# Loading the w_in groups by eight transfers that alternate between the partition halves

## The chip, the core and the metric

The kernel runs on one core of a Trainium2 chip. The metric is the device time of one execution in microseconds (us). The kernel before takes 523.92 us, the median of three runs (523.12 to 524.32).

## What is computed

An mLSTM cell (4 batches, 8 heads, 768 steps, head width 40) is followed by a feed-forward block with the activation h·cos(h). The two parts are joined by a reshape: 3,072 tokens of 320 values.

```python
for t in range(S):                        # _attn_ref, per batch and head
    m_new = np.maximum(f_gate[:, :, t] + m, i_gate[:, :, t])
    ...
    C = f_stab * C + i_stab * outer(vt, kt)
    n = f_stab * n + i_stab * kt
    y[:, :, t] = sigmoid(o_gate[:, :, t]) * (C @ qt) / np.maximum(np.abs(n @ qt), 1.0)
x = attn_out.transpose(0, 2, 1, 3).reshape(B * S, H * D)
h = x @ w_in                              # 3072x320 by 320x2048
out = (h * np.cos(h)) @ w_out             # 2048x320
```

The two weight matrices arrive as 64-bit floats. The kernel makes 32-bit floats of them on the chip, by work on the bits.

## The kernel before

**Work and order.** The steps are cut into six chunks of 128 (`c`), and a cell is one batch of one chunk, so there are 24 cells. `first_cells` does the four cells of chunk 0 and starts the weights. After that the cells of chunk c+1 are done in between the feed-forward products of chunk c. These products go by pairs of hidden tiles: `f2` from 0 to 7, each with two tiles of 128 hidden units (`e` = 0, 1). `Up(c, f2)` multiplies the chunk's 512 tokens by the pair's columns of w_in (L726 and L720 in chunk 0), the activation follows (`near` L733 on ScalarE, `rest` L736 on VectorE, `sin` L741 on ScalarE, `gate` L745 on VectorE), and `down` multiplies the result by the pair's rows of w_out (L757). In later chunks both products run in half arrays (L670). The order is written out by hand (`first_cells`, `first_period`, `both_parts`), and each engine goes through its instructions in that order.

**Weights.** `weights_in(f)` fetches one of four groups of w_in, 512 columns, for two `f2`. The 320 rows of w_in are 8 heads of 40. The first 32 rows of the heads go to the tile `bits` (128 partitions, 2 slots i, 512 columns of 8 bytes): four transfers (L180), one for each 32 partitions `a`, each with both slots, 64 rows of 4,096 bytes, 256 KB. The last 8 rows of the heads, 64 rows in all, go to the tile `low`: the even tile of a pair to partitions 0 to 63, the odd one to 64 to 127, by four transfers (L185) of 64 rows of 1,024 bytes. `weights_in` returns three pieces: slot 0, slot 1 and low. Each piece is turned into floats by `take_apart` (ScalarE, L158 and L160), `bound` (VectorE, L164 and L165) and `put_together` (VectorE L171, then GpSimd L172). `weights_out(p)` fetches two tiles of w_out by one transfer of 640 KB to all 128 partitions (L191), which is turned by the same functions. The f-th group is asked for at L987, L1047, L1076 and L1143. The second w_out piece, the one that `down(0, 1)` needs, is asked for at L1066, behind group 1, the load of E for cell 5 (L1064) and the eight transfers of the output gate (`load_o(1)`, L1065).

**Transfers.** Nearly all transfers are issued by SyncE (SP), in program order. Until cell 6 or so (`at_once`), `transfer` issues at once (L320). The DMA completions of SP are counted on eight semaphores that take turns, so an issue can stand behind the landing of the transfer eight places earlier. `load_o(c)` fetches the output gate by eight transfers, two (`g`) for each 32 partitions `a`. `load_E(n)` fetches the decay exponents, 128 partitions of 4,096 bytes, and, for even cells, `G` by two transfers of 64 partitions.

Of the kernel before, what the change touches and what calls it, by code (L numbers as in the profile page):

```python
# [12 lines left out]
I32 = mybir.dt.int32  # L13
# [16 lines left out]
def kernel(  # L30
# [20 lines left out]
    nc = tc.nc  # L51

    B, H, S, D = q.shape
# [3 lines left out]
    HP = H // 2  # L57
# [6 lines left out]
    NK = DM // 128  # L64
# [71 lines left out]
    w_in_sb = wp.tile([128, NK, DFF], FP, name="w_in_sb")  # L136
# [5 lines left out]
    WP, WQ = 512, 2 * DM  # L142
    w_out_bits = moe_w_out.bitcast(I32).rearrange("r (n two) -> r n two", two=2)
    w_in_heads = moe_w_in.bitcast(I32).rearrange("(a e d) m -> a d e m", e=NK, d=D)
# [27 lines left out]
        nc.gpsimd.tensor_tensor(out=t, in0=t, in1=m, op=OP.add)  # L172


    w_in_last = moe_w_in.bitcast(I32).rearrange("(h d) (a e n) -> e a h d n", d=D, e=2, n=2 * 128)[:, :, :, 32:D]

    def weights_in(f):
        bits = pb.tile([128, NK, WP, 2], I32, name="bits", tag="bits")
        for a in range(HP):
            nc.sync.dma_start(out=bits[32 * a:32 * a + 32].rearrange("r i n two -> r i (n two)"),  # L180
                              in_=w_in_heads[a, 0:32, :, ts(f, 2 * WP)])
        low = p2.tile([128, 2 * 128, 2], I32, name="low", tag="S")
        for e in range(2):
            for a in range(2):
                nc.sync.dma_start(out=low[64 * e:64 * e + 64, ts(a, 128)].rearrange("r n two -> r (n two)"), in_=w_in_last[e, 2 * f + a])  # L185
        return [(w_in_sb[:, i, ts(f, WP)], bits[:, i]) for i in range(NK)] + [(w_in_l[:, ts(f, 2)].rearrange("p a n -> p (a n)"), low)]


    def weights_out(p):
        bits = pc.tile([128, 2, DM, 2], I32, name="bits", tag="bits")  # L190
        nc.sync.dma_start(out=bits, in_=w_out_bits[ts(p, 256)].rearrange("(e r) n two -> r e n two", e=2))  # L191
        return w_out_sb[:, ts(p, 2)].rearrange("p f n -> p (f n)"), bits.rearrange("p e n two -> p (e n) two")


# [100 lines left out]
    sig, xT, xL, Es, kws, qkT, pss, heads_of, raw_o, Gs, early = {}, {}, {}, {}, {}, {}, {}, {}, {}, {}, {}  # L295
# [16 lines left out]
    def transfer(out, in_, room=4):  # L312
        todo.append((out, in_, room))
        if at_once[0]:
            issue(None)

    def issue(room):
        while todo and (room is None or todo[0][2] <= room or todo[0][2] == ROOM <= room + 8):
            dst, src, took = todo.pop(0)
            nc.sync.dma_start(out=dst, in_=src)  # L320
            if room is not None:
                room -= took

    def load_o(c, bs=range(B)):
        if c == 0:
            sig[c] = og.rearrange("q b k i -> q (b k i)")[:, 0:B * DM].rearrange("q (b h d) -> q b h d", b=B, h=H)
            for b in bs:
                nc.sync.dma_start(out=sig[c][:, b], in_=o_gate[b, :, ts(c, C)].rearrange("h t d -> t h d"))
            return
        raw_o[c] = p1.tile([128, B, 2 * C // 32, D], FP, name="o", tag="o")  # L330
        src = o_gate.rearrange("b (a g) (c t k) d -> a g c t b (k d)", g=2, k=C // 32, t=32)
        for a in range(HP):
            for g in range(2):
                dst = raw_o[c][32 * a:32 * a + 32].rearrange("t b (g k) d -> t g b (k d)", g=2)[:, g]
                transfer(out=dst, in_=src[a, g, c], room=6)
# [329 lines left out]
    def both(low, high, done):  # L665

        passed = max(bank.seen if bank.half == 1 - half else 0 for half, bank, *_ in (low, high))
        for half, bank, a, lhs, rhs, start, stop in (low, high):
            r = slice(64 * half, 64 * half + 64)
            ins = nc.tensor.matmul(a, lhs[r], rhs[r], start=start, stop=stop).ins  # L670
            if passed:
                tc.add_manual_dep(ins, over[passed - 1].name, SYNC, reason="a bank passes from one half to the other")
            bank.half, bank.seen = half, len(over) + 1
        if done:
            over.append(nc.sync.nop().ins)
            tc.add_manual_dep(over[-1], ins.name, SYNC, reason="the halves are done with their banks")
# [5 lines left out]

    spare_bank = 1

    class Up:


# [6 lines left out]
        def split(self, c, f2):  # L694
            banks = [Bank(pu) for pu in self.pu]

            def product(half, e, i, start=False):
                pu = self.pu[e]
                if i < NK:
                    return (half, banks[e], pu.rearrange("p (b t) -> p b t", b=B), w_in_sb[:, i, ts(2 * f2 + e, 128)],  # L700
                            xT[c][:, i:NK * B:NK], start, False)
                return half, banks[e], pu, w_in_l[:, f2], xL[c].rearrange("p b t -> p (b t)"), False, True

            for i in range(NK):
                both(product(0, 1, i, i == 0), product(1, 0, i, i == 0), i == NK - 1)
            if f2 == 3:
                send_kept()
            apart(c, f2)
            issue(24 if f2 % 2 else 32)
            for i in range(NK + 1):  # L710
                both(product(0, 0, i), product(1, 1, i), False)

        def whole(self, c, f2):

            ahead = f2 % 2 == 1 and c < NC - 1

            def low():
                for e, pu in enumerate(self.pu):
                    r = slice(64 * e, 64 * e + 64)
                    nc.tensor.matmul(pu, w_in_l[r, f2], xL[c][r].rearrange("p b t -> p (b t)"), start=ahead, stop=not ahead)  # L720

            if ahead:
                low()
            for i in range(NK):
                for e, pu in enumerate(self.pu):
                    nc.tensor.matmul(pu.rearrange("p (b t) -> p b t", b=B), w_in_sb[:, i, ts(2 * f2 + e, 128)], xT[c][:, i:NK * B:NK],  # L726
                                     start=(i == 0 and not ahead), stop=(i == NK - 1 and ahead))
            if not ahead:
                low()
# [50 lines left out]
    def send_kept():  # L780
        while kept:
            dst, src = kept.pop(0)
            transfer(out=dst, in_=src, room=5)
# [135 lines left out]
    def apart(c, f2):  # L919

        if f2 == 1 and c > 1:
            late_of[c - 1] = late_products(c - 1)
            run(late_of[c - 1], 2)
        else:
            d = c if f2 else c - 1
            run_to(d, done[d] + (2 if c in (1, NC - 1) or f2 % 2 else 3))
# [28 lines left out]
    def first_cells():  # L955
# [5 lines left out]
        load(0, "v")  # L961
        load(1, "qk")
        load_o(0, (0, 1))
        load(1, "v")
        load(2, "qk")
# [17 lines left out]
        load(2, "v")  # L983
        load_E(3)
        load_o(0, (2, 3))
        load(3)
        pieces.extend(weights_in(0))  # L987
        wall_in(1, 0, psum_o())
        wall_in(1, 1, psum_o())
# [36 lines left out]
        seam(1)  # L1026
        load_two(B, "Kv")
        outs.append((0, weights_out(0)))
        weigh(2)
        decay_exponents(3)  # L1030
# [14 lines left out]
        put_together(*pieces.pop(0))  # L1045
        values(3)
        pieces.extend(weights_in(1))  # L1047
        seam_out(2)
        state(2)
# [13 lines left out]
        put_together(*pieces.pop(0))  # L1063
        load_E(B + 1)  # L1064
        load_o(1)  # L1065
        outs.append((1, weights_out(1)))  # L1066
        load_E(B + 2)
        outs.append((2, weights_out(2)))
        low_dimensions(B)
        turn_blocks(B)  # L1070
# [3 lines left out]
        odd_values(B)  # L1074
        scale_q(B)
        ahead.append(weights_in(2))  # L1076

    spot = const.tile([1, 1], FP, name="spot")
# [240 lines left out]
```

## Time and profile before

| | us |
|---|---|
| median of three runs | 523.92 |
| the profiled execution | 523.49 |
| its span, first to last instruction | 521.4 |
| around the span (523.49 - 521.4) | 2.1 |
| PE busy | 500.7 (96% of the span) |
| DVE, ACT, POOL busy | 405.1, 285.5, 247.6 |
| mean granted PE clock | 0.991 |

PE is TensorE's matmuls, PEld its weight loads, DVE is VectorE, ACT ScalarE, POOL GpSimd, SP SyncE and SPq its queue of DMA issues. In the waits, "A <- B: x, n, y" says that A stood idle for x us in n places, y at the longest, until B. In the timelines the columns are start, duration, engine, line, operation, tiles, count, and in brackets the idle time before and what ended it. In the view by stages, each row has the length, each engine's busy time, the granted PE clock, the DMA engines' busy share and GB/s. Besides these views the trace keeps each DMA packet with its start, size and duration; 16 DMA engines work side by side.

The transfers named above, in the page's list:

```profile
E<-M_d SPq DMA_DIRECT2D x22, 512.0 KB, 3.9
...
bits<-in_moe_w_out_dram SPq DMA_DIRECT2D x8, 640.0 KB, 4.4
bits<-in_moe_w_in_dram SPq DMA_DIRECT2D x16, 256.0 KB, 7.7
```

The last column is the median time from issue to landing in us.

### The profile page before, as it was taken

The page shows a single profiled execution, that of the slowest core. Times are in us where ns is not written, and L with a number is a line of the kernel's source. Part 1 is how long each engine was busy: PE and PEld are TensorE (multiplying, and loading weights), DVE is VectorE, ACT ScalarE, POOL GpSimd, SP SyncE. Part 2 cuts the span into 40 slices and gives each one's busy share as a digit, 9 for nine tenths or more (in the row PEclk, how much of TensorE's full clock was granted, in tenths as well). Part 3 has the DMA queues.
Part 4 walks back from the last instruction along what each step waited for, and adds up shares of the span by engine and source line. Part 5 has one row for each costly group of instructions (what it writes and reads, how often), then busy time and mean ns, then how long its engine had stood idle before and what let it go on. Part 6 is the DMA issues. An engine that isn't in the chain of part 4 may idle for free.

```text
span 521.4 us, 14075 instructions
## 1 busy us (share of the span) xinstructions
PE 500.7 (96%) x5568; PEld 360.6 (69%) x5568; DVE 405.1 (78%) x826; ACT 285.5 (55%) x547; POOL 247.6 (47%) x411
## 2 busy tenths in 40 slices
PE   6999869899999999999999999999999999999995
PEld 3874446555667877877767777767787677677775
DVE  4888589897778887898887898877888778654644
ACT  2797498767575446836437837437827532222230
POOL 7536455555665866544564544563432433122212
PEclk9999988999999999999999999999999999999998
DMA  9999899999721645543534454634563000001001
GB/s 138 216 190 190 209 224 213 250 188 240 136 97 31 140 80 145 121 69 90 137 93 115 100 119 112 161 80 105 123 110 106 1 7 6 1 1 52 1 1 52
DMA packets 97777, 58.04 MB, mean 111 GB/s; under 512 B 62048, under 2 KB 89792, under 8 KB 97712
## 3 DMA queue, kind: packets, MB, share of 16 engines
q1 hardware_dynamic: 95952, 55.31, 49.5%
q0 software_dynamic: 1424, 1.49, 1.2%
q8 instruction: 44, 0.72, 0.6%
q10 hardware_dynamic: 336, 0.34, 0.2%
q14 instruction: 21, 0.17, 0.1%
HBM read 51.71 MB, written 4.11 MB: 107 GB/s over the span
## 4 chain that ended last, share of the span: by engine, by line
PE 81%; DMA 10%; DVE 3%; SPq 1%; POOL 1%; issue 1%; ACT 1%; DVEq 0%; POOLq 0%
PE pup L670 32%; PE acc L670 24%; DMA bits<-in_moe_w_in_dram 4%; PE late L670 4%; PE ps L499 3%; PE po L757 3%; DMA E<-M_d 3%; PE pup L726 3%; PE vt L534 2%; PE vt L525 2%; DMA ks<-in_k_dram 2%; DMA qr<-in_q_dram 1%; PE pu L626 1%; PE pup L720 1%; PE pw L953 1%
## 5 line engine op out<-in xcount | busy, mean ns | idle before, releaser
L733 ACT ACTIVATE n<-pup 128x512 int32<-128x512 f32 x96 | 52.3, 593 | 182.1 <-PE pup L670 165.8
L670 PE MATMUL pup<-xT,w_in_sb 64*128 64x512 f32 x608 | 148.2, 596 | 0.2 <-DVE g L745 0.2
L736 DVE SCALAR_TENSOR_TENSOR n<-pup,n 128x512 f32<-128x512 f32 x96 | 61.9, 686 | 73.3 <-ACT n L733 73.2
L670 PEld LDWEIGHTS pup<-xT,w_in_sb 64*128 64x128 f32 x608 | 60.1, 187 | 35.0 <-issue 31.8
L811 POOL TENSOR_TENSOR D<-g 128x128 f32<-128x128 f32 x40 | 18.9, 472 | 132.1 <-DVE g L745 122.8
L741 ACT ACTIVATE n<-n 128x512 f32<-128x512 f32 x96 | 58.9, 630 | 17.5 <-DVE n L736 17.5
L670 PE MATMUL acc<-w_out_sb,g 64*128 64x160 f32 x624 | 63.7, 297 | 0.0
L745 DVE SCALAR_TENSOR_TENSOR g<-pup,n 128x512 f32<-128x512 f32 x96 | 62.2, 681 | 1.4
L670 PE MATMUL acc<-T,g 64*128 64x160 f32 x624 | 61.7, 296 | 0.0
L670 PEld LDWEIGHTS acc<-w_out_sb,g 64*128 64x128 f32 x624 | 55.7, 187 | 8.3 <-issue 8.1
L670 PEld LDWEIGHTS acc<-T,g 64*128 64x128 f32 x624 | 54.1, 187 | 9.6 <-issue 8.9
L632 POOL DMA_DIRECT2D xL<-xT x40 | 22.4, 561 | 63.9 <-DVE xT L562 49.5
L430 ACT ACTIVATE E<-E,tab 128x128 f32<-128x128 f32 x160 | 49.0, 388 | 0.2
L757 PE MATMUL po<-w_out_sb,g 128*128 128x320 f32 x128 | 37.6, 449 | 3.7 <-POOL w_out_sb L172 3.7
L670 PE MATMUL pup<-xL,w_in_l 64*128 64x512 f32 x152 | 40.3, 589 | 0.0
L670 PE MATMUL acc<-T,S 64*128 64x160 f32 x312 | 39.5, 296 | 0.0
L670 PE MATMUL acc<-w_out_sb,S 64*128 64x160 f32 x312 | 39.2, 296 | 0.0
L726 PE MATMUL pup<-xT,w_in_sb 128*128 128x512 f32 x80 | 36.8, 602 | 1.5 <-DVE g L745 1.4
L757 PEld LDWEIGHTS po<-w_out_sb,g 128*128 128x128 f32 x128 | 24.9, 197 | 16.2 <-POOL w_out_sb L172 4.5
L499 PEld LDWEIGHTS ps<-t,t 40*128 40x128 f32 (+1 forms) x384 | 25.3, 188 | 11.3 <-DVE t L480 5.7
L670 PEld LDWEIGHTS acc<-w_out_sb,S 64*128 64x128 f32 x312 | 30.4, 187 | 3.1 <-issue 3.1
L670 PEld LDWEIGHTS late<-w_out_sb,D 64*128 64x128 f32 x320 | 28.7, 187 | 4.9 <-issue 4.2
(199 smaller groups left out, 958.6 us busy)
## 6 DMA issues: line engine op xcount, KB each, us to landing
E<-M_d SPq DMA_DIRECT2D x22, 512.0 KB, 3.9
qr<-in_q_dram SPq DMA_DIRECT2D x36, 160.0 KB, 3.6
kr<-in_k_dram SPq DMA_DIRECT2D x36, 160.0 KB, 5.5
G<-G_d SPq DMA_DIRECT2D x20, 256.0 KB, 5.6
bits<-in_moe_w_out_dram SPq DMA_DIRECT2D x8, 640.0 KB, 4.4
bits<-in_moe_w_in_dram SPq DMA_DIRECT2D x16, 256.0 KB, 7.7
out_dram<-o_sb SPq DMA_DIRECT2D x22, 160.0 KB, 3.8
ks<-in_k_dram SPq DMA_DIRECT2D x10, 320.0 KB, 7.1
```

Source lines behind the costliest of these rows:

```text
L430: nc.scalar.activation(out=Es[n][:, h], in_=Es[n][:, h], func=AF.Exp, scale=-1.0, bias=tab[:, c, 0, g:g + 1])
L499: nc.tensor.matmul(ps[j][:, p], kT[r, p], qT[r, p], start=True, stop=True)
L525: nc.tensor.matmul(vt[32 * a:32 * a + 32, i], vs(n)[:, h, 0:32], E[:, h], start=True, stop=False)
L632: nc.gpsimd.dma_start(out=xL[c][64 * e:64 * e + 64, b], in_=ys[n][0:128:2])
L670: ins = nc.tensor.matmul(a, lhs[r], rhs[r], start=start, stop=stop).ins
L726: nc.tensor.matmul(pu.rearrange("p (b t) -> p b t", b=B), w_in_sb[:, i, ts(2 * f2 + e, 128)], xT[c][:, i:NK * B:NK], start=(i == 0 and not ...
L733: nc.scalar.activation(out=self.n[e], in_=self.pu[e], func=AF.Copy, bias=0.25)
L736: nc.vector.scalar_tensor_tensor(out=self.n[e].bitcast(FP), in0=self.pu[e], scalar=0.25, in1=self.n[e], op0=OP.add, op1=OP.subtract)
L741: nc.scalar.activation(out=r, in_=r, func=AF.Sin, scale=TWO_PI_DOWN)
L745: nc.vector.scalar_tensor_tensor(out=g, in0=self.pu[e], scalar=TWO_PI, in1=self.n[e].bitcast(FP), op0=OP.mult, op1=OP.mult)
L757: nc.tensor.matmul(po[c][b], gs[c, f][:, ts(b, C)], w_out_sb[:, f], start=(f == 0), stop=(f == NF - 1))
L811: tt(out=D1, in0=G0[:, 1, 1], in1=G1[:, 1, 1], op=OP.add)
```

## The change

The heads' rows of a group come by eight transfers in place of four, slot 0 first, and within a slot in the order 0, 2, 1, 3 of the partition groups, so that consecutive transfers write partitions 0-31, 64-95, 32-63, 96-127. Each is 32 rows of 4,096 bytes, 128 KB. The last rows come by two transfers of 64 rows of 2,048 bytes in place of four of 1,024. For this the two tiles of a pair are chosen otherwise: in each group of four, the first goes with the third and the second with the fourth. `part_of` gives the place of such a tile in `w_in_sb`, and `weights_out` fetches the rows of w_out in the same pairs, by as many rows of the same size. `load_o` takes the partition groups in the order 0, 2, 1, 3 too. Nothing that TensorE, VectorE, ScalarE or GpSimd computes changes in number or shape.

```diff
-    w_in_last = moe_w_in.bitcast(I32).rearrange("(h d) (a e n) -> e a h d n", d=D, e=2, n=2 * 128)[:, :, :, 32:D]
+    w_in_last = moe_w_in.bitcast(I32).rearrange("(h d) (f e n) -> e f h d n", d=D, e=2, n=4 * 128)[:, :, :, 32:D]
...
-        for a in range(HP):
-            nc.sync.dma_start(out=bits[32 * a:32 * a + 32].rearrange("r i n two -> r i (n two)"),
-                              in_=w_in_heads[a, 0:32, :, ts(f, 2 * WP)])
+        for i in range(NK):
+            for a in (0, 2, 1, 3):
+                nc.sync.dma_start(out=bits[32 * a:32 * a + 32, i].rearrange("r n two -> r (n two)"),
+                                  in_=w_in_heads[a, 0:32, i, ts(f, 2 * WP)])
...
-            for a in range(2):
-                nc.sync.dma_start(out=low[64 * e:64 * e + 64, ts(a, 128)].rearrange("r n two -> r (n two)"), in_=w_in_last[e, 2 * f + a])
+            nc.sync.dma_start(out=low[64 * e:64 * e + 64].rearrange("r n two -> r (n two)"), in_=w_in_last[e, f])
...
-        nc.sync.dma_start(out=bits, in_=w_out_bits[ts(p, 256)].rearrange("(e r) n two -> r e n two", e=2))
+        src = w_out_bits[ts(p // 2, 512)].rearrange("(e a r) n two -> a r e n two", e=2, a=2)
+        nc.sync.dma_start(out=bits, in_=src[p % 2])
...
-        for a in range(HP):
+        for a in (0, 2, 1, 3):
             for g in range(2):
...
+    def part_of(f2, e):
+        return 4 * (f2 // 2) + 2 * e + f2 % 2
...
-                    nc.tensor.matmul(pu.rearrange("p (b t) -> p b t", b=B), w_in_sb[:, i, ts(2 * f2 + e, 128)], xT[c][:, i:NK * B:NK],
+                    nc.tensor.matmul(pu.rearrange("p (b t) -> p b t", b=B), w_in_sb[:, i, ts(part_of(f2, e), 128)], xT[c][:, i:NK * B:NK],
```

More of the change, by code (lines that the diff above doesn't have):

```diff
@@ L699, in product @@
                 if i < NK:
-                    return (half, banks[e], pu.rearrange("p (b t) -> p b t", b=B), w_in_sb[:, i, ts(2 * f2 + e, 128)],
+                    return (half, banks[e], pu.rearrange("p (b t) -> p b t", b=B), w_in_sb[:, i, ts(part_of(f2, e), 128)],
                             xT[c][:, i:NK * B:NK], start, False)
```

## Prediction

> **What bounds the kernel now.** I read the page's slices first, then PE's timeline, then the waits of the stretch where PE has holes, and last SP's queue and the DMA rates.
>
> ```profile
> PE   6999869899999999999999999999999999999995
> ...
> DMA  9999899999721645543534454634563000001001
> ```
>
> A slice is 13 us. PE is full from slice 8 to the last but one. Its holes are in slices 4, 5 and 7 (52 to 104 us), and there the DMA engines are full. So what transfers cost can only show before about 100 us. PE's timeline has the four holes:
>
> ```profile
> 59.81 3.88 PE L726 MATMUL pup<-xT,w_in_sb 128*128 128x512 f32 x8 [1.44 <-DVE g L745]
> ...
> 68.43 6.03 PE L757 MATMUL po<-w_out_sb,g 128*128 128x320 f32 x16 [3.69 <-POOL w_out_sb L172]
> ...
> 77.42 0.43 PE L525 MATMUL vt<-E,vs 128*32 128x128 f32 x8 [1.87 <-DVE E L505]
> ...
> 95.38 1.13 PE L720 MATMUL pup<-xL,w_in_l 64*128 64x512 f32 x4 [1.76 <-POOL w_in_l L172]
> ```
>
> They add up to 8.8 us. The clock is another loss: the L757 group takes 6.03 us here and 4.47 us elsewhere, and the stages 64 to 84 us have a granted clock of 0.83. So some 10 to 12 us, 2%, is all that any transfer could give. The waits say what stands behind the holes:
>
> ```profile
> ACT w_out_sb L158 <- DMA bits<-in_moe_w_out_dram: 4.8, 1, 4.8
> ...
> PE po L757 <- POOL w_out_sb L172: 3.7, 1, 3.7
> ...
> ACT w_in_sb L158 <- DMA bits<-in_moe_w_in_dram: 3.4, 1, 3.4
> ...
> POOL E L416 <- DMA E<-M_d: 2.2, 1, 2.2
> ```
>
> The decisive one is the first. ACT waits to 63.98 us for the second w_out piece; from there its timeline has no idle time over 0.3 us until 85 us, and the holes at 77.42 and 95.38 hang on that chain. So whatever brings this piece earlier by x moves the whole stretch from 64 to 95 us by x, and PE, full afterwards, keeps it. SP's queue shows why the piece is late:
>
> ```profile
> 44.55 1.75 SPq L180 DMA_DIRECT2D bits<-in_moe_w_in_dram  x4
> 46.35 2.63 SPq L185 DMA_DIRECT2D low<-in_moe_w_in_dram  x4
> 49.35 0.35 SPq L320 DMA_DIRECT2D E<-M_d  x1
> 50.70 8.84 SPq L320 DMA_DIRECT2D o<-in_o_gate_dram  x8
> 59.58 0.43 SPq L191 DMA_DIRECT2D bits<-in_moe_w_out_dram  x1
> ```
>
> The eight output gate issues take 8.84 us though one is 0.31 us: each stands until the transfer eight places earlier has landed (50.70 is behind a head transfer that landed at 50.68, 59.58 behind the gate transfer that landed at 59.49; SP's waits name w_in's transfers 10 times, 8.0 us). Behind that are the DMA engines, whose rate depends on the partitions written:
>
> ```profile
> 46.20:47.10 0.90, 0.90 (x9) 0.29 (x10) 0.90 (x2) 0.32 (x1) 0.90 (x2) 1.00 1.03 412
> 48.30:49.50 1.20, 1.20 (x62) 1.13 (x55) 1.16 (x3) 1.20 (x3) 1.20 (x2) 1.00 1.00 201
> 49.70:50.30 0.60, 0.60 (x4) 0.00 (x0) 0.56 (x2) 0.26 (x1) 0.01 (x1) 1.00 1.12 266
> 50.40:51.40 1.00, 1.00 (x5) 0.52 (x4) 0.97 (x2) 0.00 (x0) 0.00 (x0) 1.00 1.07 213
> ```
>
> The last figure is GB/s. The first row is w_out alone, to 128 partitions: 412. The second is group 1's heads in partitions 0 to 63, the fourth those in 64 to 127: 201 and 213. The third is the moment in which the engines pass, one by one, from one half to the other: 266. In packets of 4,096 bytes: 159 ns for E (63 to 64 us), 322 ns within a half, 274 ns in that passage. G, 64 partitions at once, has 292 ns, so the limit lies in the half.
>
> **The change, part by part.**
> *Heads.* 256 packets a group stay. Unmixed they take 256 x 322 / 16 = 5.15 us, fully mixed 256 x 159 / 16 = 2.54 us, so the gain is between 0 and 2.6 us a group. Today there is one passage. What it is worth: in group 1, 39 packets at 274 ns against 325 save 39 x 51 / 16 = 0.12 us; in group 2, 76 at 300 against 323, 0.11 us; in group 3, 73 at 293 against 320, 0.12 us. The order 0, 2, 1, 3, twice, has seven passages: six more, 6 x 0.12 = 0.7 us a group. I take 0.7, the nearest row; an engine that is ahead should stay ahead by as much.
> The Trainium skill ("SBUF — State Buffer", section "Can I just issue two DMAs to hit both halves?") speaks against it: two concurrent DMAs at partitions 0 and 64 were only 6% faster than one, "they serialize". By that, estimated, a group gains 0.3 us and not 0.7. The 266 row shows some mixing, between 0% and the 100% that 412 would be.
> *Last rows.* The same bytes in half as many packets. 1,024 bytes take 73 to 85 ns; 2,048 lie between that (a gain of 0.6 us a group, if a packet's cost were fixed) and twice that (none). At 4,096 the time is set by bytes, 322 ns or 79 ns per 1,024, so I take 0.1 us.
> *SP.* Two low issues of 0.60 us go, four head issues of 0.43 come: +0.5 us a group, by these rows. At 44.55 us 640 KB of w_out still lie ahead in the DMA engines (their packets run to 47.2), and at 62.47 us E, G and a w_out piece; this backlog hides it. Without it, it costs 0.5 us each time. Of the eight places, ten transfers now fill more, but each lands earlier: E then stands behind the third head transfer of 128 KB, which ends with the data of today's first 1.5 of 256 KB.
> *Output gate, order 0, 2, 1, 3.* E and the first four gate transfers today share half 0: 256 KB of E and 4 x 80 KB; these go on from 53.6 to 57.3 us. With two of the four in the other half, 160 KB leave it, 0.8 us at 201 GB/s. Between 0 (E's slow packets have another reason) and 3 us (E at 159 ns: 128 x 159 / 16 = 1.3 us from 53.6 and some 1.2 to land, 56.1 in place of 59.2). I take 0.8. The last gate issue, just ahead of w_out, stands behind E's landing (59.2 us).
> *Slots.* The first piece needs four of eight transfers. ACT's 3.4 us wait and the 1.44 us hole go; but PE then waits as much longer for w_out at the next hole, so by itself this is worth 0.
> *Pairs, part_of, w_out's rows.* As many packets of the same size, same matmuls: 0. The pairs stay in one group, so no product waits for a later group.
>
> Sum up to the second w_out piece: groups 0 and 1, 2 x (0.7 + 0.1) = 1.6, and 0.8 for E, 2.4 us, less 0.2, my share of rival 2's 0.5 for the thin backlog at 44 us (a DMA busy share of 0.16): **2.2 us**. Group 0 counts because the engines are full from 23 to 44 us. The holes at 77.42 and 95.38 move along: groups 2 and 3 are 0.8 us faster each, so their data do not become late (group 2's lands at 75.76 us, when ACT wants it, and half of it is now enough). The profiled execution gives 523.49 - 2.2 = 521.3 us; the median of the runs lies 0.4 above that execution, which I leave in the range.
>
> **Rivals.**
> 1. *No mixing*: the 16 engines go in step through each half. Then heads gain 0, E's and w_out's issues stay, only the 1.44 us hole moves into the next: 523.5 us. For it: within a half all 16 packets have the same 310 to 345 ns, so the engines are nearly in step. Against it: the 266 row in all three groups.
> The Trainium skill's 6% (the section named above) would lead near this: estimated, 2 x 0.3 = 0.6 us, 522.9 us.
> 2. *Slower*: SP becomes the bound. If the DMA engines have run dry when a group is issued, the added 0.5 us is on the path, and at four groups it makes up to 2.1 us: 525.6 us, or 524.5 at two. It decides if the busy share is under about 0.5 when the first head is issued. For it: it is 0.16 at 44 us and 0.37 at 59 us. Against it: it is 1.0 elsewhere, and w_out's 640 KB go ahead of groups 1 to 3.
> The Trainium skill ("DMA: Bandwidth & Descriptors", section "Rules for kernel authors") asks for transfers of 1 MiB and more. With its fixed 2 us, four more transfers in single file would, estimated, cost 8 us a group; here eight are in flight, issued 0.4 us apart, and no run yet shows transfers of 128 KB.
> 3. *More*: once an engine is ahead, it writes alone into the other half and the lead grows to full mixing: 2.6 + 0.1 us a group, 5.4 for two, plus 0.8: 6.2 us, less what ACT and PE hold back. PE's work from 49 us on is without holes to 58.4 and from there needs 4.7 us for the next product, so w_out can come no more than about 5 us earlier to effect: 518.5 us; a half-clock window less (1.6 us), 517.
>
> **How the numbers follow.** Forecast (1 to 3.5 us less) 0.46; more (rival 3) 0.20; no mixing 0.19; slower 0.15. What a measurement of this kernel can tell from no change is about 0.2%, 1 us. Faster is the forecast and rival 3, 0.66; same is rival 1, 0.19; slower 0.15. The range leaves out the far end of rival 3 and of rival 2: 517.5 to 524.6. It takes in both ends of the heads' cost.
>
> **What would show it.** Head packets after the change at about 275 ns (0.7 us a group); 322 would be rival 1, 160 to 200 rival 3. The w_out issue that was at 59.58 should be near 57.4, and ACT's 3.4 us wait for w_in gone. PE's L757 hole should end near 66.2 in place of 68.43, with PE full from about 93. I am wrong if the DMA engines show gaps behind the new head issues, or if the w_out piece is earlier and ACT's chain from 64 to 85 us is not.

## The result and the profile after

| | before | changed |
|---|---|---|
| median (20 runs of each, in turn) | 523.12 us | 519.99 us |
| lowest to highest | 520.95 to 525.03 | 517.85 to 524.33 |
| ratio, with its 95% interval | 1 | 0.995 (0.9934 to 0.9965) |
| profiled execution (its span) | 523.49 us (521.4) | 520.97 us (519.1) |
| mean granted clock in it | 0.991 | 0.989 |

The change takes 2.6 us (0.005 x 523.12; from 1.8 to 3.5 by the interval). The forecast was 2.2. The two medians themselves lie 3.1 apart. The two profiled executions lie 2.52 us apart.

The page of the changed kernel, its slices and its chain of work that ended last:

```profile
PE   6999987999999999999999999999999999999994
...
DMA  9999999999332553642633653633652000001001
...
PE 87%; DVE 8%; ACT 2%; issue 1%; POOL 1%; DMA 0%; DVEq 0%
```

Counted from 0, PE has 8 and 7 in slices 5 and 6 and is full elsewhere in the first hundred microseconds; before it had 8, 6 and 8 in slices 4, 5 and 7. DMA's slice 10 fell from 7 to 3: the first burst ends earlier. In the chain the share of DMA is 0%; in the page of before it is 10% of the span. So in this execution the transfers are no longer in the chain that ended last. That is not the change alone: in a second profile of each kernel, described below, their share is 7% before and 5% changed. PE's timeline of the changed kernel, 58 to 94 us (start, length, and in brackets the idle time before):

```profile
58.35 3.67 PE L730 MATMUL pup<-xT,w_in_sb 128*128 128x512 f32 x8 [0.25 <-DVE g L749]
...
63.91 4.58 PE L761 MATMUL po<-w_out_sb,g 128*128 128x320 f32 x16 [0.83 <-POOL w_out_sb L172]
...
71.77 0.43 PE L526 MATMUL vt<-E,vs 128*32 128x128 f32 x8 [2.03 <-DVE E L506]
...
84.77 3.67 PE L730 MATMUL pup<-xT,w_in_sb 128*128 128x512 f32 x8 [1.62 <-DVE g L749]
90.31 1.13 PE L724 MATMUL pup<-xL,w_in_l 64*128 64x512 f32 x4 [1.86 <-POOL w_in_l L172]
91.67 2.08 PE L500 MATMUL ps<-t,t 40*128 40x128 f32 x16 [0.24 <-DVE t L481]
93.68 6.81 PE L761 MATMUL po<-w_out_sb,g 128*128 128x320 f32 x16
```

(Lines of PE's code stand four higher: L757 is now L761.) The 1.44 us hole is 0.25, the 3.69 us hole is 0.83, the two later ones stayed, and one of 1.62 us is new. The holes add up to 8.76 us before (the four of the prediction) and to 6.6 after (0.25, 0.83, 2.03, 1.62 and 1.86). The last two rows show what was given back: L500 takes 2.08 us and L761 6.81, where the same groups took 1.16 and 4.58 before, 3.15 us in all. The granted clock is at half from 91.4 to 98.2 us in this execution. In the first profile of before it is at half for just as long, but in two stretches of 3.4 us, from 68.0 and from 78.2 us; behind each of them PE still comes to a hole (77.42 and 95.38), which can take up a delay, while PE is full behind 98 us. SP's queue, the same kernel:

```profile
40.29 4.26 SPq L181 DMA_DIRECT2D bits<-in_moe_w_in_dram  x8
44.84 1.35 SPq L185 DMA_DIRECT2D low<-in_moe_w_in_dram  x2
46.23 0.44 SPq L321 DMA_DIRECT2D E<-M_d  x1
46.71 7.08 SPq L321 DMA_DIRECT2D o<-in_o_gate_dram  x8
53.85 0.42 SPq L192 DMA_DIRECT2D bits<-in_moe_w_out_dram  x1
```

The heads and the last rows together stand 5.61 us on SP (4.26 + 1.35) where it was 4.38 (1.75 + 2.63), yet w_out's second piece goes out at 53.85 in place of 59.58. The rate at which group 2's heads flow, in the view by stages (the last figure is GB/s, the one ahead of it the DMA busy share, ahead of that the granted clock), first before, then changed:

```profile
69.20:73.00 3.80, 3.80 (x12) 2.54 (x11) 3.73 (x6) 3.77 (x10) 1.59 (x4) 0.71 1.04 213
```

```profile
63.40:66.60 3.20, 2.69 (x10) 1.98 (x11) 2.96 (x8) 3.17 (x10) 0.46 (x1) 1.00 1.04 255
```

213 became 255 GB/s with all engines busy in both.

### The profile page after: what moved, and what is told of

The parts are those of the page before. It is cut to its first block, busy times and chain, and to the rows that moved or that the text cites. A ratio compares the mean times of both kernels' runs of the same rounds, so it can differ in the third digit from the quotient of the medians.

```text
span 519.1 us, 14096 instructions
## 1 busy us (share of the span) xinstructions
PE 500.6 (96%) x5568; PEld 362.2 (70%) x5568; DVE 405.2 (78%) x826; ACT 285.4 (55%) x547; POOL 247.9 (48%) x411
## 4 chain that ended last, share of the span: by engine, by line
PE 87%; DVE 8%; ACT 2%; issue 1%; POOL 1%; DMA 0%; DVEq 0%
PE pup L671 32%; PE acc L671 24%; PE po L761 5%; PE late L671 4%; PE pup L730 4%; PE ps L500 4%; PE vt L535 2%; PE vt L526 2%; PE pup L724 1%; PE pw L957 1%; PE pu L627 1%; PE ph L516 1%; PE vt L529 1%; PE vt L532 1%; DVE t L481 1%
## 5 line engine op out<-in xcount | busy, mean ns | idle before, releaser
L737 ACT ACTIVATE n<-pup 128x512 int32<-128x512 f32 x96 | 52.3, 593 | 186.6 <-PE pup L671 165.8
L761 PE MATMUL po<-w_out_sb,g 128*128 128x320 f32 x128 | 38.5, 457 | 0.8 <-POOL w_out_sb L172 0.8
L761 PEld LDWEIGHTS po<-w_out_sb,g 128*128 128x128 f32 x128 | 25.2, 200 | 14.2 <-issue 3.2
L500 PEld LDWEIGHTS ps<-t,t 40*128 40x128 f32 (+1 forms) x384 | 26.5, 193 | 10.6 <-DVE t L481 5.5
```

The costliest lines, as they stand in the source:

```text
L500: nc.tensor.matmul(ps[j][:, p], kT[r, p], qT[r, p], start=True, stop=True)
L737: nc.scalar.activation(out=self.n[e], in_=self.pu[e], func=AF.Copy, bias=0.25)
L761: nc.tensor.matmul(po[c][b], gs[c, f][:, ts(b, C)], w_out_sb[:, f], start=(f == 0), stop=(f == NF - 1))
```

## The experiments

The theory: the seven passages between the partition halves make the heads faster, and with them the w_out piece earlier (M, mixing). Rivals: that it is the size and number of the transfers (S); that the gain lies in the gate's order or the last rows; and, for what is lost again, that the half clock at 91 us hides some 3 us (H).

One measure is used in all runs: the mean time of a 4,096-byte head packet, group by group, over the 160 packets that go before the first packet of the last rows (from the trace's DMA records). Another is the issue of the second w_out piece on SP, and a third the start of PE's first product of chunk 1 (the first matmul into `acc`, L867 in the changed kernel; the line differs by a few).

| kernel | passages a group | ratio (95%) | packets, groups 0 to 3 (ns) | w_out issue (us) | products start (us) |
|---|---|---|---|---|---|
| before | 1 | 1 | 293, 311, 312, 306 | 59.58 | 151.53 |
| before_again | 1 | one time: 522.16 us | 279, 311, 317, 309 | 57.34 | 150.19 |
| changed | 7 | 0.995 (0.9934 to 0.9965) | 197, 259, 253, 237 | 53.85 | 148.80 |
| changed_again | 7 | 0.9933 (0.9908 to 0.9958) | 210, 252, 249, 224 | 56.10 | 147.73 |
| heads_halves_apart | 1 | 1.0001 (0.998 to 1.0022) | 305, 308, 305, 277 | 56.97 | 148.95 |
| heads_in_order | 3 | 0.9969 (0.9948 to 0.999) | 258, 286, 281, 285 | 57.56 | 151.81 |
| heads_four_alternating | 3 | 0.9987 (0.9967 to 1.0007) | 274, 282, 288, 267 | 59.38 | 151.14 |
| heads_alone | 7 | 0.9953 (0.9929 to 0.9977) | 234, 246, 226, 220 | 54.47 | 146.54 |
| heads_and_gate | 7 | 0.9935 (0.991 to 0.9961) | 225, 242, 233, 226 | 55.52 | 150.17 |
| gate_order_alone | 1 | 0.9983 (0.9963 to 1.0004) | 270, 307, 316, 304 | 57.43 | 151.66 |
| last_rows_alone | 1 | 1.0015 (0.9995 to 1.0036) | 283, 302, 310, 287 | 57.79 | 150.02 |
| last_rows_alternate | 7 | 1.001 (0.9994 to 1.0026) | 205, 245, 282, 204 | 56.87 | 149.32 |
| heads_sixteen | 15 | 1.0151 (1.0131 to 1.017) | 223, 240, 239, not taken | 64.64 | 159.37 |
| warm_in_holes | 7 | 0.9961 (0.9946 to 0.9975) | 234, 242, 230, 248 | 57.36 | 149.08 |

**heads_in_order**: the changed kernel with the four slots of each tile in the plain order, so that a group has three passages.

```
-            for a in (0, 2, 1, 3):
+            for a in (0, 1, 2, 3):
```

> The changed kernel with the heads' eight transfers in the order 0, 1, 2, 3 within each slot: three passages between the halves in place of seven; number, size and slots of the transfers stay. Theory M (passages between the halves make the gain): head packets of 4,096 bytes go back from about 255 ns to about 300 ns in groups 1 to 3, the second w_out piece is issued 1 to 1.5 us later than in the changed kernel (53.85 us), and the time is about 521.5 us. Theory S (smaller transfers land one by one, so SP's eight places come free earlier, mixing or not): issue near 54, time as the changed kernel, 520.0 us.

Measured: 521.21 us, ratio 0.9969, packets of 281 to 286 ns in groups 1 to 3: between one passage and seven in both. The w_out issue, expected 1 to 1.5 us later than in the changed kernel, came 3.7 us behind its first profile and 1.5 behind its second.

**heads_halves_apart**: the changed kernel's eight transfers, first all of half 0 and then all of half 1.

```
-        for i in range(NK):
-            for a in (0, 2, 1, 3):
+        for a in range(HP):
+            for i in range(NK):
```

> The changed kernel with the eight head transfers in the order of the kernel before (partitions 0-31 slot 0, 0-31 slot 1, 32-63 slot 0, and so on): one passage between the halves, still eight transfers of 128 KB. Theory M: head packets near 320 ns, second w_out piece issued at about 56 to 57 us, time about 522 us. Theory S: as the changed kernel, 520.0 us. If it comes out at 523 or more, the smaller transfers themselves cost something that mixing pays back.

Measured: 522.65 us, ratio 1.0001. The heads of group 2 flow at 221 GB/s:

```profile
66.80:70.20 3.40, 3.40 (x10) 2.22 (x10) 3.33 (x5) 3.37 (x10) 1.41 (x3) 0.71 1.06 221
```

This keeps the eight transfers, the gate's order and the last rows, but neither the alternation nor the first slot ahead of the second, and it gains nothing that can be measured. S falls in so far as it is about size and number: twice as many transfers of half the size, with the gate's order and the last rows, bring no gain that shows, and no loss. That slot 0 comes first is not separated from the alternation here; no run has seven passages without it.

**gate_order_alone**: before, with the output gate's slots in the order 0, 2, 1, 3.

```
-        for a in range(HP):
+        for a in (0, 2, 1, 3):
```

> The kernel before with only the output gate's transfers in the order 0, 2, 1, 3. My step: E shares half 0 with two gate transfers in place of four and lands 0.8 us earlier, so the second w_out piece is issued at about 58.8 us in place of 59.58, and the time is 0.5 to 0.8 us less, about 522.4 us. Rival: the gate's transfers are paced by SP's eight places and their order does nothing, 523.1 us.

Measured: 522.0 us, ratio 0.9983, which is 0.9 us less than before and fits the 0.8 of the prediction, but the interval holds no change as well. The w_out issue, expected at 58.8 us, came at 57.43; but the unchanged kernel's second profile has 57.34, so the issue shows no effect.

**last_rows_alone**: before, with the last rows in two transfers of 2,048-byte rows, and the pairs, part_of and w_out's rows that go with them.

```
-            for a in range(2):
-                nc.sync.dma_start(out=low[64 * e:64 * e + 64, ts(a, 128)]..., in_=w_in_last[e, 2 * f + a])
+            nc.sync.dma_start(out=low[64 * e:64 * e + 64]..., in_=w_in_last[e, f])
...
```

> The kernel before with only the last rows in two transfers of 64 rows of 2,048 bytes and the tiles paired first-third and second-fourth. My step: 0.1 us a group, 522.9 us, no difference that can be told. Rival L (the packets, half as many and two issues fewer, are what brings the gain): last rows done 0.6 us earlier a group and 1.2 us of SP issue less, time 521.5 us or less.

Measured: 523.66 us, ratio 1.0015. No gain, and a loss of up to 1.9 us is inside the interval.

**heads_alone**: before, with the eight alternating head transfers only. The tiles stay paired as they were.

```
-        for a in range(HP):
+        for i in range(NK):
+            for a in (0, 2, 1, 3):
...
```

> The kernel before with only the heads' eight transfers in the changed order; last rows, pairs and gate order as before. Theory M (passages between the halves): head packets about 255 ns in groups 1 to 3, the second w_out piece issued near 55 to 56 us, and nearly all of the gain: 520.5 us. Rival (the parts only work together): 522 us or more.

Measured: 520.17 us, ratio 0.9953, as much as the whole change within the intervals. Its heads of group 2 reach 286 GB/s:

```profile
63.40:67.00 3.60, 3.46 (x13) 2.51 (x14) 3.36 (x8) 3.59 (x9) 0.56 (x2) 1.00 1.03 286
67.00:70.00 3.00, 2.28 (x21) 1.42 (x19) 2.15 (x4) 2.69 (x5) 2.84 (x7) 1.00 0.52 153
```

The second row is the stretch right behind them: the DMA engines are only half busy, while SP issues the four transfers of the last rows (66.00 to 68.63 us in its timeline) and then q's and k's.

**heads_four_alternating**: the changed kernel, with four head transfers of 256 KB in the order 0, 2, 1, 3, that is three passages without smaller transfers.

```
+        for a in (0, 2, 1, 3):
+            nc.sync.dma_start(out=bits[32 * a:32 * a + 32].rearrange("r i n two -> r i (n two)"),
+                              in_=w_in_heads[a, 0:32, :, ts(f, 2 * WP)])
```

> The changed kernel with the heads in four transfers of 256 KB as before, in the order 0, 2, 1, 3: three passages between the halves, as in heads_in_order, but four issues less a group and no slot ahead of the other. Theory M: by its passages like heads_in_order, 521.3 us, head packets about 285 ns. Rival S (it is the smaller transfers and the first slot's earlier landing): 522.9 us, as last_rows_alone and gate_order_alone together.

Measured: 522.42 us, ratio 0.9987, packets of 267 to 288 ns, as in heads_in_order. Three passages give the same packets in four transfers as in eight, and with and without slot 0 first. So the packets go as theory M said. The time does not: 522.42 us lies nearer to the rival's 522.9 than to M's 521.3, and M's number is just outside the interval (521.4 to 523.5 us). The intervals of this run and of heads_in_order, 0.9987 and 0.9969, overlap; whether the smaller transfers or the first slot's earlier landing add to the gain in time, these runs don't tell.

**heads_sixteen**: the changed kernel with each head transfer cut into two of 16 rows (64 KB).

```
+            for h in range(2):
+                for a in (0, 2, 1, 3):
+                    r = 32 * a + 16 * h
+                    nc.sync.dma_start(out=bits[r:r + 16, i]...,
+                                      in_=w_in_heads[a, 16 * h:16 * h + 16, i, ...])
```

> The changed kernel with sixteen head transfers of 16 rows (64 KB) in place of eight: fifteen passages between the halves, one packet an engine and transfer. Theory M alone: head packets near 200 ns, a further 0.7 to 0.9 us a group, time 518.5 us. My view: eight more issues a group at 0.42 us make 6.9 us of issuing for some 4 us of data, and SP's eight places hold 512 KB, so the DMA engines run dry in the groups, the second w_out piece is issued 1 to 3 us later than in the changed kernel, and the time is 521 to 523 us.

Measured: 530.99 us, ratio 1.0151: 8 us more than before, in the direction of rival 2 but far beyond what was expected. SP's queue, and the stage in which group 1 is issued:

```profile
45.59 9.57 SPq L183 DMA_DIRECT2D bits<-in_moe_w_in_dram  x16
55.60 1.35 SPq L187 DMA_DIRECT2D low<-in_moe_w_in_dram  x2
57.49 7.11 SPq L323 DMA_DIRECT2D o<-in_o_gate_dram  x8
64.64 0.43 SPq L194 DMA_DIRECT2D bits<-in_moe_w_out_dram  x1
```

```profile
50.00:57.00 7.00, 7.00 (x74) 3.86 (x64) 4.38 (x6) 2.82 (x4) 3.51 (x3) 1.00 0.37 97
```

Sixteen issues take 9.57 us. SP's waits account for little of it:

```profile
SPq L183 <- DMA bits<-in_moe_w_out_dram: 1.3, 1, 1.3
SPq L183 <- ACT n L739: 0.3, 1, 0.3
```

The other 8 us, 0.5 for each, are taken as issuing. Meanwhile the DMA engines are busy for 0.37 of the time, and the packets (240 ns) are no faster than with eight transfers. That is rival 2's mechanism: once the engines run dry, each issue is on the path. Against the changed kernel two groups have sixteen issues more, 16 x 0.5 = 8 us. The w_out issue is 9.7 us later than the mean of the changed kernel's two profiles, and by the two ratios the run lost 10.5 us to the changed kernel (0.0201 x 522.91), 8.1 to the kernel before. So the issues make up most of the loss; some 2 us of it stay open. SP decides between eight and sixteen transfers.

**last_rows_alternate**: the changed kernel with the last rows in four transfers of 32 rows that alternate between the halves too.

```
-        for e in range(2):
-            nc.sync.dma_start(out=low[64 * e:64 * e + 64]..., in_=w_in_last[e, f])
+        for j in range(2):
+            for e in range(2):
+                r = 64 * e + 32 * j
+                nc.sync.dma_start(out=low[r:r + 32]..., in_=w_in_last[e, f, 4 * j:4 * j + 4])
```

> The changed kernel with the last rows in four transfers of 32 rows of 2,048 bytes, 0-31, 64-95, 32-63, 96-127. Theory M: three passages in place of one, last rows done about 0.2 us earlier a group, against two more issues of 0.5 us: 519.8 us, not to be told from the changed kernel. If issues are what counts, 520.8 us.

Measured: 523.22 us, ratio 1.001. This was missed: the gain of the heads is gone, though their packets are fast (245, 282 and 204 ns). Behind group 2's heads the engines wait:

```profile
69.50:74.00 4.50, 1.62 (x18) 0.97 (x16) 3.42 (x6) 4.21 (x9) 4.34 (x8) 0.98 0.42 114
```

A busy share of 0.42 for 4.5 us speaks for SP's issuing. But heads_alone has as many transfers a group and 0.52 for 3 us, and keeps its gain. What makes the difference is not settled.

**heads_and_gate**: before, with the heads and the gate's order, without the last rows and the pairing.

```
-        for a in range(HP):
+        for i in range(NK):
+            for a in (0, 2, 1, 3):
...
-        for a in range(HP):
+        for a in (0, 2, 1, 3):
```

> The kernel before with the heads' eight transfers and the gate's order of the changed kernel, but the last rows in four transfers of 1,024-byte rows and the tiles paired as before. By the ratios so far (heads alone 0.9953, gate alone 0.9983, last rows alone 1.0015) it should be the fastest of all, 0.9936, 519.7 us; if the last rows' two issues less are worth something beside the heads' four more, it is slower than the changed kernel, 521 us.

Measured: 519.78 us, ratio 0.9935. The new pairs, part_of and w_out's rows are not needed for the gain; that they cost or give something below 1 us can't be excluded. No version here is clearly faster than the changed kernel.

**changed_again** and **before_again**: both kernels unchanged, for a second profile of each.

> The changed kernel once more, for a second profile beside the kernel before's second one. In the nine profiles so far the start of chunk 1's products is 92 us behind the issue of the second w_out piece (91.7 to 92.5), and 94.2 to 95.0 where the clock was halved for 6.8 us in one stretch. Theory M with that: issue between 54 and 57.5 us here, products 92 or 94 to 95 us behind it, time 520 us. If the issue is near 59.5 as in the first profile of the kernel before, M falls.

> The kernel before once more, for a second profile. Theory M: the second w_out piece issued at 58 to 60 us, head packets 300 to 320 ns in groups 1 to 3, chunk 1's products 92 us behind the issue, or 94 to 95 if a half clock of 6.8 us falls in between. If the issue is as early as the changed kernel's (54 to 57), the profiles differ by the execution and not by the change.

Measured: 519.75 us (0.9933) and one time of 522.16 us. SP's queue in the second profile of the changed kernel, then of before:

```profile
42.22 4.36 SPq L181 DMA_DIRECT2D bits<-in_moe_w_in_dram  x8
...
48.56 7.47 SPq L321 DMA_DIRECT2D o<-in_o_gate_dram  x8
56.10 0.42 SPq L192 DMA_DIRECT2D bits<-in_moe_w_out_dram  x1
```

```profile
49.39 7.76 SPq L320 DMA_DIRECT2D o<-in_o_gate_dram  x8
57.34 0.38 SPq L191 DMA_DIRECT2D bits<-in_moe_w_out_dram  x1
```

The same code issues w_out's second piece 2.2 us apart in two executions, in both kernels (59.58 and 57.34, 53.85 and 56.10). So one profile's shift of 5.7 us isn't the change's effect; the means are 58.5 and 55.0, 3.5 us. The expectation for before, 58 to 60 us, was missed. Over all kernels, the five profiles with one passage have a mean issue of 57.8 and the six with seven passages 55.7, which is 2.1 us, and the two ranges overlap (56.97 to 59.58 and 53.85 to 57.36).

**warm_in_holes**: the changed kernel with 15 matmuls of no use in the two holes before 91 us, into a bank that is free.

```
+            if (c, f2) == (0, 4):
+                bank = ps_a.pool.tile([128, HP, C], FP, name="pk", tag=ps_a.tags[(ps_a.turn + 1) % 2])
+                warm(7, bank)
...
+                if (c, f2) == (0, 4):
+                    warm(8, bank)
                 low()
```

> The changed kernel with 15 more matmuls on zeros (to a bank that is free then, nothing reads them) in PE's two holes before and within Up(0, 4), at about 83 and 88 us. Theory H: the changed kernel's gain at 90 us is 5 us, and some 3 us are given back because the clock is halved for 6.8 us after these holes; with the holes filled the half clock stays away and the time is 517 to 518 us. Rival: the half clock falls elsewhere or was in few executions, or the added matmuls delay as much as they save: 520 to 521 us.

Measured: 521.12 us, ratio 0.9961. The holes are filled and the clock stays full there:

```profile
85.87 1.67 PE L962 MATMUL pk<-nil 128*128 128x512 bf16 x7
90.87 1.89 PE L962 MATMUL pk<-nil 128*128 128x512 bf16 x8
92.91 1.13 PE L724 MATMUL pup<-xL,w_in_l 64*128 64x512 f32 x4 [0.15 <-POOL w_in_l L172]
...
95.45 4.57 PE L766 MATMUL po<-w_out_sb,g 128*128 128x320 f32 x16
```

L766 takes 4.57 us in place of 6.81, and yet the median isn't lower. In this execution w_out went out at 57.36, 3.5 us later than in the first changed profile and 1.3 later than in the second. H, that 3 us wait to be recovered there, falls as far as the median goes. A late issue in one execution can't be all of it: the nine runs of this kernel all have a mean clock of 0.992 or more and a median of 521.1 us, while the changed kernel's runs with 0.990 or more have 519.6. The added matmuls seem to cost about what the full clock saves; where they do is not shown.

## Why the prediction was right, step by step

**What bounds the kernel.** It held. In all 14 profiles the time from the start of chunk 1's products to the end of the span is 369.9 to 370.9 us, whatever was changed. And the products start 91.6 to 92.9 us behind the issue of the second w_out piece in nine profiles, 94.2 to 95.0 in the other five, all of which have a stretch of 6.8 us at half clock behind or across that issue (the first changed profile: 148.80 - 53.85 = 95.0; the second: 147.73 - 56.10 = 91.6; before: 91.95 and 92.85). So the issue does move all behind it, as the chain argument said, less 2 to 3 us where the clock falls to half for 6.8 us in one stretch.

**Heads: right in kind, mis-sized.** The step priced a passage at 0.12 us and six of them at 0.7 us a group. Measured, with 256 packets on 16 engines: group 0, (286 - 203) x 16 = 1.3 us; group 1, (311 - 255) x 16 = 0.9; group 2, 1.0; group 3, 1.2 (means of two profiles each). In groups 1 to 3 one passage more is worth 0.17 to 0.21 us in the five kernels with seven (65 to 80 ns x 16 / 6, against 311 ns), and 0.22 to 0.26 in the two with three; the kernels with one passage differ among themselves by 0.2 us a group, so both are rough, the latter above all. I had counted only packets that ran while the engines were on both sides; a passage is worth about half as much again as that. Whether the lead of some engines lasts behind a passage, as rival 3 had it, is a reading, not shown; full mixing (159 ns) came nowhere, with 15 passages it was 223 to 240.

**Output gate, 0.8 us.** Fits gate_order_alone (0.9 us) but is not resolved from nothing, and the step by which it was to come, an earlier w_out issue, does not show there: from group 1's first issue to the w_out piece it takes 14.18 us, against 15.03 and 14.23 in the two profiles of before.

**Last rows, 0.1 us a group.** Nothing of it shows (1.0015), and heads_and_gate does without. (322 ns for 4,096 bytes are 80.5 for 1,024, not the 79 of the prediction; nothing hangs on it.)

**SP, 0.5 us a group, hidden.** Without SP's waits (1.0 us in the heads of group 1) a head issue takes 3.26 / 8 = 0.41 us, as priced, and heads_halves_apart, with all these issues, stands at 1.0001: within its interval of about 1 us either way it was hidden. The backlog is near its end: heads_alone shows half idle engines behind the heads, heads_sixteen the full price.

**Slots.** As said: ACT's 3.4 us wait for w_in's bits is gone, and the 1.44 us hole with it. The waits of the changed kernel, 39 to 100 us (us in total, times, longest):

```profile
PE pup L730 <- DVE g L749: 1.9, 2, 1.6
...
ACT w_out_sb L158 <- DMA bits<-in_moe_w_out_dram: 1.9, 1, 1.9
...
PE po L761 <- POOL w_out_sb L172: 0.8, 1, 0.8
```

ACT waits 1.9 us for the w_out piece in place of 4.8.

**The sum.** 2.2 us were forecast for the piece and for the end. On the mean of two profiles each the piece moved by 3.5 us and the end by 2.6, with 2.2 us between two executions of one code. The terms are not where the forecast had them. In SP's queue, group 1's first issue comes 2.6 us earlier on the mean (44.55 and 43.11 before, 40.29 and 42.22 changed), and from there to the piece it takes 0.9 us less (15.03 and 14.23, 13.56 and 13.88). The sum had 0.8 us for the first part, which is group 0, and 1.4 for the second (0.8 for group 1, 0.8 for the gate, less 0.2). Nearly all of the first part is won in one issue that the prediction did not name: that of `vs`, ahead of group 1. In the two profiles of before, then in the two of the changed kernel:

```profile
33.61 8.11 SPq L320 DMA_DIRECT2D vs<-in_v_dram  x1
...
33.66 7.78 SPq L320 DMA_DIRECT2D vs<-in_v_dram  x1
...
43.11 1.75 SPq L180 DMA_DIRECT2D bits<-in_moe_w_in_dram  x4
```

```profile
32.73 4.72 SPq L321 DMA_DIRECT2D vs<-in_v_dram  x1
...
33.76 5.69 SPq L321 DMA_DIRECT2D vs<-in_v_dram  x1
```

In all five profiles with one passage this issue takes 7.8 to 8.1 us, in all six with seven 4.7 to 7.2. What it stands for, the traces don't say. Over all profiles with one and with seven passages the two parts are 1.4 and 0.8 us, so their sizes are uncertain by about a microsecond, but both times the first is the larger. So the forecast's nearness to the measured 2.6 us is partly luck: the path up to the piece was right, but group 0's term was too small, the rest too large, and a loss to the clock was not in the sum.

Part of the difference between the piece's 3.5 us and the end's 2.6 is in two things that the prediction had not: one is the half clock. The other is DVE. I had ACT's chain from the w_out piece to 85 us move as a block, without a gap; that block ends just ahead of a gap of 1.69 us in the kernel before (ACT's L741 at 88.20 us waits for DVE's L736), and in the first changed profile the gap at this place is longer:

```profile
79.16 1.05 ACT L737 ACTIVATE n<-pup 128x512 int32<-128x512 f32 x2
83.15 1.23 ACT L745 ACTIVATE n<-n 128x512 f32<-128x512 f32 x2 [2.94 <-DVE n L740]
```

DVE is busy for 8.10 of the 8.40 us from 74 to 82.4 there and comes late, which is the new hole of 1.62 us on PE. In the second changed profile this hole is not there.

**Signs.** Head packets of about 275 ns were expected; 255, 251 and 231 came in groups 1 to 3, faster than that but not rival 3's 160 to 200. The L757 hole, expected to end near 66.2 us, ends at 63.91 and 65.03 in the two profiles. Of the signs of being wrong, gaps of the DMA engines behind the new head issues show weakly: behind group 2's heads their busy share is 0.76 from 66.60 to 69.00 us in the first profile and 0.96 from 68.90 to 71.00 in the second. The other sign stayed away: in the first profile ACT's chain moved with the piece, from 63.98 to 58.01 us at its start and from 85.05 to 79.16 at its last step (L733, now L737).

**Rivals.** Rival 1 (no mixing) is refuted by the packets. It stood beside a sentence of the Trainium skill ("SBUF — State Buffer", section "Can I just issue two DMAs to hit both halves?"): 6% for two DMAs, "they serialize". Here the trace disagrees: eight queued transfers in alternation flow at 255 GB/s in place of 213, 20% more. Rival 2 (SP) did not decide here, but does at 16 transfers. Rival 3 (full mixing) did not come.

## What to carry to other kernels

Where transfers to half the partitions bound a stage, issue them so that neighbours in the queue write different halves; the time of a packet goes with the number of passages, and these can be counted before it is tried. Faster packets alone are no gain yet: last_rows_alternate had them and heads_four_alternating had some of them, and neither kernel's time is clearly lower. Cut no finer than the issuing engine can feed: look at the DMA busy share right behind the new issues, and stop when it falls. Profile the same code twice before a shift of 2 us is read as an effect.

## What the runs showed of the hardware that was not expected

The granted clock goes with more than half as much time as the change. In the runs of the kernel before that went with the experiments (three sets), those with a mean clock of 0.990 or more have a median of 522.2 us (34 runs), those below 523.7 (46); in the changed kernel 519.6 (16) and 521.1 (4). The 1.5 us between them is more than half of what the change gives. In each of the two groups the changed kernel is 2.6 us faster, so the gain itself is not the clock's, as far as runs of different sets can be compared. Why the stretch at half clock is 6.8 us in five profiles and 3.4 in the others, with nearly the same holes ahead of it, these runs don't show: warm_in_holes took the stretch away, and its nine runs, all at 0.992 or more, are not faster for it. The Trainium skill ("TensorE: Matmul & The Clock Gate", section "Part 1: The HAM clock gate") has the chip look at the load in a window of about 3.4 us that runs freely of the kernel; stretches of 3.4 and 6.8 us, at other places in each profile of the same code, agree with that.
